# An attention and token-mixing block on one core: raw projection weights for the first two chunks, statistics, norms and weight scalings on any of three engines, and another instruction order

## The chip, the core and the metric

The kernel runs on one core of a Trainium2 chip. The metric is the device time of one execution in microseconds. The engines are PE (TensorE: matmuls, and transposes as matmuls), PEld (its weight loads, which overlap it), DVE (VectorE), ACT (ScalarE), POOL (GpSimd) and SP (SyncE, which here only issues DMAs; its queue shows as SPq). Each engine works through its own queue in order and waits for others by semaphores.

## What is computed

x has 2048 rows (tokens) of 512. Six vectors (sa, ca, ga, sb, cb, gb) come from `silu(c) @ w_mod`. Then:

```
h = layernorm(x) * (1 + ca) + sa
x = x + ga * attention(h)          # 32 heads of 16; each row sees itself and 7 rows before it, 2 apart
h = layernorm(x) * (1 + cb) + sb
x = x + gb * mixer(h)              # layernorm, then an MLP across the 2048 rows: w1 to 1792, gelu, w2 back
```

Attention projects h with wqkv to q, k and v, forms 8 logits per row and head, takes a softmax over them, weights 8 rows of v and projects with wo. Everything in and out is bfloat16.

## The kernel before

Rows lie in 16 tiles of 128. Attention works in five chunks of 2, 4, 4, 4 and 2 tiles (256, 512, 512, 512, 256 rows). `build_chunk` (line 616) creates the operations of a chunk; every operation has a name, and the names are used below.

- `ld_x...` load x, `ld_wqkv0/1/2` the weights of q, k and v (512 KB each), `ld_wmod...` those of the six vectors. `modcols1` and `a1col` make the column 1 + ca, `modcols0` and `sab` the column sa.
- `ln1s` (line 370) is a tile's mean and variance: bn_stats and bn_aggr on DVE, or two accumulating passes on ACT and a short DVE operation `ln1v`. `rstd` takes the inverse deviation on ACT for a group of tiles, `nb` on DVE the matching shift, `n1_t` (`ln_norm`, line 404) normalizes tile t into the tile `h`. The same three steps stand for the second norm (`ln2q`, `ln2m`, `n2_t`) and the third (`ln3s`, `h3_t`); `aff` between them applies cb and sb with two DVE operations.
- `tr` transposes the normalized tiles of chunks 0 and 1 on PE into PSUM and `hT` copies them out; chunks 2 to 4 are transposed by DMA (`xt`).
- `wsc{t}_{kt}` (`scale_w`, line 435) multiplies a quarter of a q, k or v weight matrix by 1 + ca into `w_qkv`. The shift by sa goes through `qvb`, a bias column per projection.
- `qkv{ch}_{t}{j}` projects (t is 0 for q, 1 for k, 2 for v), `ev` evicts the result. `vd` are DMAs that spread v.
- `qk` (DVE) multiplies q by the 8 shifted k, `red` (PE) sums over a head, `max`, `sub`, `exp`, `esum`, `rcp` and `smB` are the softmax, `a2` are DMAs that spread its result, `pv` (DVE) multiplies it by v, `pvacc` (PE) sums, `oev` evicts, `wo` projects, `x1` writes the new x. A qk or pv product of a 512-row chunk is one DVE operation on 4096 elements per partition with both inputs in SBUF (the tile `big`).
- `mlp1` multiplies by w1, `park` keeps partial sums, `padd` and `gelu` finish, `mlp2` multiplies by w2 and `fin` writes out.

The order of the work is written out by hand in the string `ORDER` (lines 182 to 238): a list of the names, in which each engine finds its own queue. A suffix chooses the engine (`:a` ACT, `:d` DVE, `:p` POOL), `:q` splits each matmul of an operation into four that use 32 columns each, and `fill` and `warm` are matmuls without a use, put where PE would stand idle. `schedule` (line 85) turns the string into instructions and gives out the buffers: six PSUM banks, four `big`, five `vD`. Which engine a norm runs on was fixed by three strings of letters, `NE`; which statistics ran on ACT by `LN1A`; which weight scalings on POOL by `VPOOL`.

All operations are recorded by one helper, so that the profile shows them under one line (L133); its rows are told apart by the tiles they write and read.

Of the kernel before, what the change touches and what calls it, by code (L numbers as in the profile page):

```python
# [187 lines left out]
hT1_3:a qkv0_00 sab ev0_12:d n1_6 ld_wmod4 qvb0 ln1s14 ld_wo1 qkv0_02 qvb_cp0 ln1s15 ev0_00:a wsc2_2 qvb1
wsc2_0:d qkv1_00 wsc2_3 ev0_10:a ev0_02:d ln1s10 wsc2_1:d qkv1_10 qvb_cp1 qk0_0 ev1_10:a qkv0_22 qk0_1 n1_7
qkv0_20 ln1s13 qk0_2 qkv1_02 xt6 red0_0 ev1_00:a qk0_3 red0_1 red0_2 ev0_22:a ld_wmod5 qkv1_22 qk1_0 ev0_20:a  # L190
qkv1_12 ev1_02:a vd0_1 red0_3 ev1_12:a mask qkv1_11 vd0_0 ln1s11 max0 xt8 qk1_2 qkv1_01 ev1_11:a sub0 qkv1_03
ev1_01:a xt9 exp0 qkv1_13 qk1_1 ev1_03:a xt7 esum0 ev1_13:a qkv1_20 rcp0 vd0_2 ln1s12 qkv1_21 smB0 qk1_3 a2_0_3
modcol2 rstd1_4 qkv1_23 a2_0_0 ev1_22:a a2_0_2 halo_v1:a red1_0 ev1_20:a a2_0_1 red1_1 ln1v10 ln1v12 ln1v11
ln1v13 nb1_4 red1_2 rstd1_3 n1_15 ld_wo3 red1_3 nb1_3 ld_wo2 mcols0 n1_11 n1_10 qkv2_00 max1 ev1_21:a n1_14 xt10
qkv2_02 ev2_00:a pv0_0 qkv2_10 n1_12 ld_wo0 pv0_1 qkv2_11 vd0_3 ev2_10:a ev2_02:a qkv2_12 qk2_0 n1_13 qkv2_01
xt12 ev2_12:a pvacc0_0 ev2_01:a sub1 qk2_2 xt13 qkv2_03 exp1 qkv2_13 xt11 ev2_11:a ev2_03:a qkv2_22 qk2_1
ev2_13:a esum1 ev1_23:a qkv2_21 rcp1 vd1_2 red2_0 smB1 ev2_21:a ld_b2 red2_1 qk2_3 halo_v2:a a2_1_1 red2_2
# [10 lines left out]
warm3 n2_2 ev4_10:a ln3s0 wo6 a2_3_0 n2_3 ln3s1 a2_3_1 rstd2_4 wo7 x1_6 vd3_1 aff2 rstd3_0 a2_3_2 biascols wo9:q
ev4_20:a a2_3_3 nb2_4 nb3_0 ln3s3 n2_5 n2_4 vd3_2 warm1 ln3s2 h3_1 h3_0 qkv4_12 aff4 rstd3_2 wo8 x1_7 ld_w2_0
nb3_2 ln3s5 h3_3 h3_2 ln2q6 ln3s4 mlp1_0_6_0 ev4_12:a pv3_0 mlp1_0_3_0 x1_9 rstd3_4 mlp1_0_5_0 x1_8 mlp1_0_0_0  # L210
biascols_cp:a ln2q8 nb3_4 pv3_1 halo_v4:a mlp1_0_2_0 h3_4 vd4_1 h3_5 mlp1_0_1_0 ln2q9 pv3_2 ld_w2_1 mlp1_0_2_4
vd4_2 ln2q7 mlp1_0_0_4 vd4_0 mlp1_0_3_4 park0_0:a mlp1_0_1_4 mlp1_0_5_4:q park0_1:a ln2m6 vd4_3 pv3_3 park0_2:a
pvacc3_0 pvacc3_1 oev3_0:a ld_w1_0_1152 pvacc3_2 oev3_1:a mlp1_0_4_0:q rstd2_6 oev3_2:a qk4_2 pvacc3_3 park0_3:a
mlp1_0_7_0 oev3_3:a nb2_6 qk4_1 n2_6 mlp1_0_6_4 mlp1_0_4_4 n2_8 qk4_0 wo12:q ld_w1_0_1408 n2_7 n2_9 qk4_3 wo10:q
park0_4:a aff6 x1_12 red4_0 wo13:q ld_w2_3 park0_5:a ln2q12 red4_1 red4_2 x1_10 red4_3 wo11:q max4 ln2q10 ln3s9
x1_13 sub4:q mlp1_0_8_0:q exp4 ln3s8 ln2q13 mlp1_0_11_0 esum4 ln3s7 rcp4 mlp1_0_12_0 park0_6:a ln3s6 x1_11
mlp1_0_10_0 smB4 rstd3_6 ln2m12 a2_4_2 mlp1_0_9_0 h3_7 rstd2_12 h3_6 a2_4_3 ln2q11 h3_9 mlp1_0_8_4 ln2m13 a2_4_0
nb2_12 ln2m11 n2_12 mlp1_0_7_4 a2_4_1 ln2m10 h3_8 rstd2_10 ld_w2_4 aff12 mlp1_0_9_4 rstd2_13 rstd2_11 nb2_10
ln3s12 mlp1_0_9_8 mlp1_0_7_8 n2_10 mlp1_0_8_8 nb2_13 pv4_0 park0_7:a mlp1_0_12_4 ld_w1_0_1664 park0_8:a
mlp1_0_11_4 nb2_11 pv4_2 n2_13 mlp1_0_10_4 rstd3_12 pv4_1 park0_9:a mlp1_0_12_8 n2_11 mlp1_0_10_8 pv4_3 inj1_4  # L220
mlp1_0_11_8 ld_w1_1_0 park0_10:a pvacc4_2 ld_w1_1_640 park0_11:a pvacc4_0 nb3_12 aff11 pvacc4_1 h3_12 pvacc4_3
mlp1_0_13_0 aff10 oev4_0:a oev4_2:a aff13 mlp1_0_13_4 ln3s10 wo15 ld_w2_5 ln3s13 rstd3_10 mlp1_0_13_8 wo14 x1_15
rstd3_13 park0_12:a inj1_0 nb3_13 ln2s15 mlp1_1_0_6 nb3_10 x1_14 rstd2_15 mlp1_1_4_6 park0_13:a nb2_15 ln2s14
n2_15 inj1_3 inj1_6 ld_w1_1_896 inj1_5 mlp1_1_6_6 rstd2_14 aff15 h3_10 mlp1_1_3_6 ln3s15 mlp1_1_6_10 ln3s11
mlp1_1_0_10 rstd3_15 inj1_1 mlp1_1_1_6 park1_0:a nb3_15 h3_15 n2_14 rstd3_11 aff14 mlp1_1_5_6 h3_13 ln3s14
mlp1_1_5_10 mlp1_1_1_10 inj1_2 ld_w1_2_0 mlp1_1_2_6 h3_11 rstd3_14 park1_1:a h3_14 mlp1_1_4_10 mlp1_1_3_10
# [812 lines left out]
```

## Time and profile before

| | us |
|---|---|
| median of 3 runs | 206.46 (206.19 to 206.73) |
| profiled execution, first to last instruction (span) | 204.6 |
| PE busy | 194.7 |
| DVE busy | 163.3 |
| ACT busy | 120.6 |
| POOL busy | 13.0 |
| first projection matmul starts | 13.61 |
| first qk product starts (DVE) | 19.48 |
| last pv product ends (DVE) | 123.0 |
| last matmul ends | 201.6 |

The profile shows the profiled execution as its span; it gives no other time for it, and the median of the runs is 1.9 us above the span. A row of busy tenths cuts the span into 40 slices of 5.1 us; a 9 is 90% or more. In a timeline the columns are start, duration, engine, line, operation, tile written <- tiles read, shape and count; in brackets stands how long the engine was idle before it and what ended that. In a list of waits the columns are who waited for whom, the total, how often, and the longest. A table by stretches gives the stretch, its length, the busy time of the engine with its count of instructions, PE's granted clock, the busy share of the DMA engines, and GB/s.

### The profile page before, as it was taken

The numbers are of one execution on the slowest core, as the hardware profiler recorded it, in microseconds if no ns is written. First come the engines' busy times: TensorE is split into PE (matmuls) and PEld (weight loads), VectorE is DVE, ScalarE is ACT, GpSimd is POOL, SyncE is SP. The second block draws the span as 40 slices with busy tenths as digits, with TensorE's granted clock in tenths as the row PEclk, the third lists the DMA queues.
The fourth block names the chain that finished last, engine by engine and source line by source line (L and its number), as shares of the span: only waits on it lengthen the run. The fifth ranks groups of instructions, "written<-read, shape, count | busy, mean of one in ns | idle before, by whom it ended". The sixth has DMA issues, their size and how long they took to land.

```text
span 204.6 us, 4223 instructions
## 1 busy us (share of the span) xinstructions
PE 194.7 (95%) x1655; PEld 103.5 (51%) x1655; DVE 163.3 (80%) x260; ACT 120.6 (59%) x283; POOL 13.0 (6%) x36
## 2 busy tenths in 40 slices
PE   3999999999999997989899999999999999999994
PEld 3988554454455553554344445444444444444453
DVE  2899999999999999999999999975473204369365
ACT  2398998994666899989898876683762000000000
POOL 4122001100000001240000000100000000000000
PEclk9999999999999999999999999999999999999999
DMA  5999494646958976194975179946990930121121
GB/s 141 330 380 348 117 239 107 161 98 201 247 186 267 308 234 251 25 272 110 289 200 115 26 157 263 288 131 200 340 304 3 232 88 16 39 77 51 51 82 51
DMA packets 55111, 35.93 MB, mean 176 GB/s; under 512 B 24628, under 2 KB 52404, under 8 KB 55092
## 3 DMA queue, kind: packets, MB, share of 16 engines
q1 hardware_dynamic: 55084, 35.67, 61.4%
q8 instruction: 13, 0.21, 0.4%
q14 instruction: 6, 0.05, 0.1%
q10 hardware_dynamic: 8, 0.00, 0.0%
HBM read 22.55 MB, written 2.10 MB: 121 GB/s over the span
## 4 chain that ended last, share of the span: by engine, by line
PE 65%; DVE 20%; issue 5%; DMA 5%; SPq 3%; ACT 2%; DVEq 0%
PE psS L133 62%; DVE big L133 9%; DVE h L133 3%; PE psL L133 3%; SPq L133 3%; DVE st L133 3%; DMA wst<-in_B_w_dram 2%; DMA xx<-in_A_x_dram 2%; ACT h L133 1%; DVE mv L133 1%; DVE m L133 1%; DVE lsb L133 1%; DVE ls L133 0%; DVE nb L133 0%; DVE woq L133 0%
## 5 line engine op out<-in xcount | busy, mean ns | idle before, releaser
L133 PE MATMUL psS<-h,wst 128*128 128x512 bf16 (+1 forms) x254 | 50.7, 379 | 1.2 <-POOL h L133 0.7
L133 PE MATMUL psS<-hT,w_qkv 128*128 128x512 bf16 (+3 forms) x312 | 46.2, 339 | 0.3 <-ACT w_qkv L133 0.3
L133 PEld LDWEIGHTS <-wst 128*128 128x128 bf16 (+1 forms) x356 | 28.7, 98 | 32.2 <-issue 3.2
L133 PEld LDWEIGHTS <-w_qkv 128*128 128x128 bf16 (+1 forms) x354 | 29.5, 111 | 21.3 <-issue 3.2
L133 DVE TENSOR_TENSOR big<-a2sb,vD 128x4096 bf16<-128x4096 bf16 (+1 forms) x20 | 36.9, 1876 | 0.0
L133 DVE TENSOR_TENSOR big<-q_sb,k_f 128x4096 bf16<-128x4096 bf16 (+1 forms) x20 | 36.3, 1857 | 0.0
L133 DVE SCALAR_TENSOR_TENSOR h<-psS,bcol,rows_bc 128x512 f32<-128x512 f32 (+2 forms) x18 | 12.4, 690 | 24.4 <-PE psS L133 24.2
L133 PE MATMUL psS<-gT,big 128*128 128x512 bf16 x112 | 24.8, 379 | 0.0
L133 PEld LDWEIGHTS <-big 128*128 128x128 bf16 x144 | 12.0, 97 | 13.2
L133 PEld LDWEIGHTS <-ident 128*128 128x128 bf16 (+1 forms) x203 | 13.9, 111 | 5.9 <-issue 2.8
L133 PE MATMUL psS<-woq,o_sb 128*32 128x512 bf16 (+1 forms) x172 | 16.6, 380 | 0.0
L133 ACT ACTIVATE h<-xx,nb,rs 128x512 bf16<-128x512 bf16 x19 | 15.0, 807 | 0.8 <-DVE nb L133 0.7
L133 DVE TENSOR_TENSOR psS<-psS,gT 128x512 f32<-128x512 f32 x14 | 9.3, 696 | 7.0 <-PE psS L133 7.0
L133 ACT ACTIVATE junk<-xx 128x512 bf16<-128x512 bf16 x22 | 13.8, 626 | 0.2
L133 POOL TENSOR_SCALAR h<-xx,rs,nb 128x512 bf16<-128x512 bf16 x9 | 7.3, 813 | 101.3 <-DVE nb L133 84.0
L133 ACT ACTIVATE lv<-mv,epscol 128x1 f32<-128x1 f32 (+2 forms) x25 | 7.3, 291 | 9.3 <-DVE mv L133 8.4
L133 DVE BATCH_NORM_STATS2 st<-xx 128x6 f32<-128x512 bf16 x14 | 9.5, 678 | 4.0 <-DMA xx<-in_A_x_dram 4.0
L133 ACT ACTIVATE gT<-psS,bcol 128x512 bf16<-128x512 f32 x14 | 8.7, 688 | 6.4 <-DVE psS L133 6.4
L133 PEld LDWEIGHTS <-group 128*32 128x32 bf16 x288 | 6.8, 96 | 10.2 <-issue 4.8
L133 DVE TENSOR_TENSOR h<-h,rows_bc 128x512 bf16<-128x512 bf16 (+2 forms) x20 | 11.5, 581 | 0.5
L133 DVE TENSOR_TENSOR h<-h,xx 128x512 bf16<-128x512 f32 (+2 forms) x18 | 11.4, 633 | 0.6
L133 ACT ACTIVATE gT<-psS 128x512 bf16<-128x512 f32 x19 | 10.8, 587 | 1.6 <-PE psS L133 1.5
(94 smaller groups left out, 220.4 us busy)
## 6 DMA issues: line engine op xcount, KB each, us to landing
vD<-v_sb SPq DMA_DIRECT2D x12, 524.5 KB, 3.8
big<-in_B_w_dram SPq DMA_DIRECT2D x4, 896.0 KB, 8.2
vD<-v_sb SPq DMA_DIRECT2D x8, 268.5 KB, 3.0
wst<-in_B_w_dram SPq DMA_DIRECT2D x3, 640.0 KB, 5.3
out_dram<-h SPq DMA_DIRECT2D x15, 128.0 KB, 1.8
xx<-in_A_x_dram SPq DMA_DIRECT2D x7, 256.0 KB, 6.1
wst<-in_B_w_dram SPq DMA_DIRECT2D x2, 800.0 KB, 4.8
gT<-in_w_mod_dram SPq DMA_DIRECT2D x3, 512.0 KB, 6.1
```

The source lines that it names most:

```text
L133: r = fn(*a, **k)
```

## The change

Four things change. The projections of chunks 0 and 1 use the raw weights as loaded (`wraw`), and for these chunks 1 + ca is multiplied into the transposed tiles by the copies `hT`, which so need `a1col`; the scaled weights are still made, for chunks 2 to 4. Statistics of the first and third norm can run on DVE or ACT, norms and weight scalings on DVE, ACT or POOL, each as its name in `ORDER` says; bn_aggr becomes an operation of its own (`ln1v`, `ln2v`, `ln3v`), and the norm on DVE that took mean and deviation without `nb` is gone. The raw v weights lie in the other `h2` buffer. And the whole of `ORDER` is another one: 34 operations carry `:q` instead of 19, on PE the 70 and 16 fillers of the start become 30, 24, 12 and 10, and POOL is given 10 norms of the first kind, 9 of the second and 8 of the third, 7 weight scalings and 2 halo copies (before: 5, 4 and 2 norms, 2 scalings and 1 halo copy).

```diff
-                k, n = map(int, rest)
+                n = int(rest[0])
+                k = min((freed["ps"][i], i) for i in range(self.pools["ps"]) if held["ps"][i] is None)[1]
...
-consts ld_x_1_2 act_table ld_x0 ld_x_1_4 ld_c ld_x_2_8 ld_x1 ident ld_x_2_6 ld_wmod1 ln1s3 halo0 ld_wqkv1 cps
-ln1s2 warm2 ld_wqkv0 silu_exp ld_wmod0 ln1s0 ln1s4 ln1s1 ln1s5 rstd1_0 ld_x_4_14 nb1_0 ln1s9 rstd1_1 n1_0 n1_1
-silu_dve nb1_1 ld_wqkv2 ln1s8 fill:2:70 tr0_0 n1_2 n1_4 modcols1 ln1s7 hT0_3:a n1_5 n1_3 ld_x_3_10 hT0_2:d a1col
-hT0_0:a fill:4:16 tr1_2 wsc1_2:d ld_b1 hT0_1:a wsc1_3:d wsc1_0:a tr1_0 wsc1_1:d ln1s6 hT1_2:a ld_wmod2 qkv0_10
...
+ident ld_x_1_4 ld_x0 act_table ld_x_1_2 ln1s4:d ln1s0:d fill:30 ld_x1 ld_wmod1 ld_c fill:24 cps fill:12 fill:10
+ln1s5:a ln1s3:a ln1s1:d ld_wqkv1 ln1v1 ln1v0 rstd1_0 ln1s2:d nb1_0 ln1v5 ln1v4 silu_exp n1_0:a n1_1:p ln1v3 silu_dve
+modcols1 ln1v2 rstd1_1 nb1_1 n1_5:p n1_4:a ld_wqkv0 a1col wsc0_0:p tr0_0 hT0_0:a n1_2:d ld_x_2_6 n1_3:d consts tr1_0
+ld_wmod0 hT1_1:a tr1_2 hT1_2:a wsc0_2:p ld_x_2_8 hT0_3:d hT0_2:d halo0 hT0_1:d ld_wqkv2 wsc0_1:a ld_b1 hT1_3:d
+wsc1_2:a hT1_0:d wsc1_0:d qkv0_12 qkv0_10 ev0_12:a qkv1_10 ln1s7:d ev0_10:d ln1v7 modcols0 ln1s6:a sab:a ln1s8:d
+qkv0_02 ln1s9:d ev1_10:a qvb0 ld_wo2 ld_wmod2 ln1v6 ln1v8 qvb_cp0:d ln1v9 rstd1_2 wsc1_1:p qkv0_00 qkv1_02 ev0_02:d
+ld_wo0 ld_x_3_10 ld_x_3_12 nb1_2 qk0_3 qvb1 qkv0_22 qkv0_20 ev0_00:a ld_b2 qk0_0 n1_8:a qk0_1 qkv1_12 n1_9:p n1_6:p
+qk0_2 qvb_cp1:a wsc2_0:a ev0_22:a ev1_02:a xt6 modcol2 red0_0 red0_1 ln1s13:d n1_7:p ev0_20:a vd0_3 mcols0 qkv1_11:q
+qkv1_00:q ev1_12:a ln1s10:a wsc0_3:p qk1_2 ln1s11:a red0_2 red0_3 wsc2_3:p ev1_00:a vd0_2 xt9 xt7 mask max0 mrowt0
+qkv1_13 ln1v11 ln1v10 wsc2_1:p mrows0:a st_row0 sub0 ev1_11:a exp0 wsc1_3:p qk1_0 qkv1_01 ev1_01:a xt8 ld_row0
+qkv1_03:q ln1s12:a esum0 rcp0 qk1_1 ev1_13:a qkv1_21:q ev1_03:a ln1v12 vd0_1 ln1v13 rstd1_3 red1_0 ld_x_4_14 smB0
+a2_0_1 qk1_3 qkv2_00:q qkv2_10:q ev2_10:a nb1_3 n1_13:p ev2_00:a qkv2_11:q ev2_11:a a2_0_3 qkv1_23 ev1_23:a wsc2_2:a
+red1_1 red1_2 red1_3 ev1_21:a a2_0_0 vd0_0 a2_0_2 qkv1_20 ev1_20:a qk2_0 qkv1_22 ld_wmod3 ev1_22:a max1 sub1 qkv2_23
+qkv2_03 halo_v1:p n1_11:p pv0_2 pvacc0_2 ld_wo1 exp1 esum1 ev2_23:a rcp1 biascols biascols_cp:a ln1s15:a pv0_3 qkv2_01
+ev2_01:a pvacc0_3 ld_wo3 pv0_0 pvacc0_0 pv0_1 pvacc0_1 oev0_0:a n1_10:p qkv2_13 ev2_13:a smB1 qkv2_02:q ev2_02:a
...
+pv2_0 ev4_02:a ev3_22:a warm3 warm1 n2_5:p aff0 exp3 warm0 qkv3_20 ev3_20:a vd3_3 vd3_0 rstd2_2 nb2_2 pvacc2_3
+oev2_3:a pvacc2_0 oev2_0:a qkv4_10:q ln3s1:a pvacc2_1 qkv4_12 pv2_2 aff4 oev2_1:a ln3s0:a ln3v0 qkv4_20 pvacc2_2 ln3v1
+oev2_2:a esum3 rcp3 ld_w1_0_512 vd3_2 n2_3:p n2_2:p aff2 rstd3_0 nb3_0 smB3 h3_0:p a2_3_2 ln3s3:d warm2 ev4_20:a
+ln3s2:d ln3v3 ln3v2 ln3s5:d wo8:q ln3s4:a ev4_12:a a2_3_1 h3_1:p wo7 rstd3_2 nb3_2 h3_2:p a2_3_0 wo9:q ev4_10:a x1_8
+a2_3_3 ln3v4 ln3v5 rstd3_4 h3_3:d qk4_3 nb3_4 vd3_1 x1_9 halo_v4:d vd4_2 h3_5:d ld_w2_2 pv3_0 h3_4:a wo6:q mlp1_0_0_0
...
+mlp1_0_0_4 pv3_3 mlp1_0_3_0 park0_0:a mlp1_0_1_4 rstd2_6 nb2_6 n2_7:p park0_1:a n2_8:p mlp1_0_2_0 mlp1_0_2_4 park0_2:a
+pvacc3_1 mlp1_0_3_4:q oev3_1:a pvacc3_0 oev3_0:a n2_9:p pvacc3_3 mlp1_0_4_0:q mlp1_0_4_4:q pv3_2 qk4_1 pvacc3_2
...
+nb2_13 n2_13:d aff13 nb2_12 mlp1_0_8_4 mlp1_0_8_8 rstd2_11 nb2_11 mlp1_0_9_0 mlp1_0_9_4 mlp1_0_9_8 n2_12:p a2_4_0
+pv4_2 pv4_0 inj1_1 ld_w1_0_1664 park0_8:a park0_9:a ln3s13:a inj1_5 mlp1_0_10_4 mlp1_0_12_8 mlp1_0_10_8 park0_10:a
...
-    NE=('PAPAAPAADAAPAAPD', 'PAPAAPAAAADAAADP', 'APPAAADDDDADAADA'),
-    LN1A=(10, 11, 12, 13),
+    RAW=(0, 1),
...
-    VPOOL=(2, 3),
...
     def ln_stats(l, st, src, reads, name):
         st6, mv = ln_t["st6", l], ln_t["mv", l]
-        if l == 0 and st in LN1A:
-            def fa():
-                nc.scalar.activation(junk[:], src, ACT.Identity, scale=1.0 / D, accum_out=mv[:, st, 0:1])
-                nc.scalar.activation(junk[:], src, ACT.Square, scale=D ** -0.5, accum_out=st6[:, st, 0:1])
-            add("act", 1.36, fa, reads=reads + ["act_table"], writes=[("sq", l, st)], name=name)
-            add("dve", 0.15, lambda: nc.vector.scalar_tensor_tensor(
-                mv[:, st, 1:2], mv[:, st, 0:1], mv[:, st, 0:1], st6[:, st, 0:1], op0=ALU.mult, op1=ALU.subtract,
-                reverse1=True), reads=[("sq", l, st)], writes=[("mv", l, st)], name="ln1v" + name[4:])
-            return
 
         def fd():
             nc.vector.bn_stats(st6[:, st, :], src)
-            nc.vector.bn_aggr(mv[:, st, :], st6[:, st, :])
-        return add("dve", 0.86, fd, reads=reads, writes=[("mv", l, st)], name=name)
+
+        def fa():
+            nc.scalar.activation(junk[:], src, ACT.Identity, scale=1.0 / D, accum_out=mv[:, st, 0:1])
+            nc.scalar.activation(junk[:], src, ACT.Square, scale=D ** -0.5, accum_out=st6[:, st, 0:1])
+        o = G.add_any([("dve", 0.68, fd)] + ([("act", 1.26, fa)] if l != 1 else []),
+                      reads=reads + (["act_table"] if l == 0 else []), writes=[("stt", l, st)], name=name)
+
+        def fv():
+            if o.eng == "dve":
+                nc.vector.bn_aggr(mv[:, st, :], st6[:, st, :])
+            else:
+                nc.vector.scalar_tensor_tensor(mv[:, st, 1:2], mv[:, st, 0:1], mv[:, st, 0:1], st6[:, st, 0:1],
+                                               op0=ALU.mult, op1=ALU.subtract, reverse1=True)
+        add("dve", 0.15, fv, reads=[("stt", l, st)], writes=[("mv", l, st)], name=name[:3] + "v" + name[4:])
 
...
-        if vreads is None and NE[l][g0:g0 + n] == "D" * n:
-            return
...
     def ln_norm(l, g0, n, st, dst, src, reads, writes, name, by_sums=False):
-        rs, nb, mv = ln_t["rs", l], ln_t["nb", l], ln_t["mv", l]
-        r_, n_, e = rs[:, st, 0:1], nb[:, st, 0:1], NE[l][st]
-        reads = reads + [("rs", l, g0)]
-        with_nb = by_sums or NE[l][g0:g0 + n] != "D" * n
-        reads.append(("nb", l, g0) if with_nb else ("mv", l, st))
-        args = (r_, n_, ALU.mult, ALU.add) if with_nb else (mv[:, st, 0:1], r_, ALU.subtract, ALU.mult)
-        alts = {"A": ("act", 0.8, lambda: nc.scalar.activation(dst, src, ACT.Identity, scale=r_, bias=n_)),
-                "D": ("dve", 0.42, lambda: nc.vector.tensor_scalar(dst, src, args[0], args[1], op0=args[2], op1=args[3])),
-                "P": ("pool", 0.8, lambda: nc.gpsimd.tensor_scalar(dst, src, args[0], args[1], op0=args[2], op1=args[3]))}
-        G.add_any([alts[e]], reads=reads, writes=writes, name=name, locks=True)
+        r_, n_ = ln_t["rs", l][:, st, 0:1], ln_t["nb", l][:, st, 0:1]
+        G.add_any([("act", 0.8, lambda: nc.scalar.activation(dst, src, ACT.Identity, scale=r_, bias=n_)),
+                   ("dve", 0.42, lambda: nc.vector.tensor_scalar(dst, src, r_, n_, op0=ALU.mult, op1=ALU.add)),
+                   ("pool", 0.8, lambda: nc.gpsimd.tensor_scalar(dst, src, r_, n_, op0=ALU.mult, op1=ALU.add))],
+                  reads=reads + [("rs", l, g0), ("nb", l, g0)], writes=writes, name=name, locks=True)
 
...
-            wst[0][:, 0:KT * D].rearrange("p (k n) -> p k n", k=KT), h2_r[0][:, 0:KT, :])
-    wkey = ([("wst", 2)], [("wst", 0)], [("h2", 0, i) for i in range(MT)])
+            wst[0][:, 0:KT * D].rearrange("p (k n) -> p k n", k=KT), h2_r[1][:, 0:KT, :])
+    wkey = ([("wst", 2)], [("wst", 0)], [("h2", 1, i) for i in range(MT)])
...
             alts = [("dve", 0.36, lambda d_=d_, s_=s_, a_=a_: nc.vector.tensor_scalar_mul(d_, s_, a_)),
-                    ("act", 0.7, lambda d_=d_, s_=s_, a_=a_: nc.scalar.activation(d_, s_, ACT.Identity, scale=a_))]
-            if t == 2 and kt in VPOOL:
-                alts = [("pool", 0.8, lambda d_=d_, s_=s_, a_=a_: nc.gpsimd.tensor_scalar(
-                    d_, s_, a_, 0.0, op0=ALU.mult, op1=ALU.add))]
+                    ("act", 0.7, lambda d_=d_, s_=s_, a_=a_: nc.scalar.activation(d_, s_, ACT.Identity, scale=a_)),
+                    ("pool", 0.8, lambda d_=d_, s_=s_, a_=a_: nc.gpsimd.tensor_scalar(
+                        d_, s_, a_, 0.0, op0=ALU.mult, op1=ALU.add))]
             G.add_any(alts, reads=wkey[t] + ["a1col"], writes=[("w_qkv", t, kt)], name=f"wsc{t}_{kt}")
...
-                    copy2(hT[:, kt, :], lambda s_=s_, k2=k2: ps(s_).bitcast(BF)[:, k2 * C:(k2 + 1) * C], C, True, [],
-                          [("hT", bh, kt)], f"hT{ch}_{kt}", frees=s_)
+                    hs = lambda s_=s_, k2=k2: ps(s_).bitcast(BF)[:, k2 * C:(k2 + 1) * C]
+                    hd, a_ = hT[:, kt, :], a1col[:, kt:kt + 1]
+                    if ch not in RAW:
+                        copy2(hd, hs, C, True, [], [("hT", bh, kt)], f"hT{ch}_{kt}", frees=s_)
+                        continue
+                    G.add_any([("act", _t_act(C, 1), lambda hd=hd, hs=hs, a_=a_: nc.scalar.activation(
+                        hd, hs(), ACT.Identity, scale=a_)),
+                               ("dve", 0.12 + 0.00052 * C, lambda hd=hd, hs=hs, a_=a_: nc.vector.tensor_scalar_mul(
+                                   hd, hs(), a_))], reads=["a1col"], writes=[("hT", bh, kt)], name=f"hT{ch}_{kt}",
+                              frees=s_)
...
-                        lhsT = _ap(w_r[t][:, kt, j:j + 1], [[4, P]])
+                        lhsT = _ap((wraw if ch in RAW else w_r)[t][:, kt, j:j + 1], [[4, P]])
...
-                reads=hkeys + [("w_qkv", t, kt) for kt in range(KT)] + [("hT_raw", bh)], alloc=s_,
+                reads=hkeys + (wkey[t] if ch in RAW else [("w_qkv", t, kt) for kt in range(KT)]) + [("hT_raw", bh)],
+                alloc=s_,
```

More of the change, by code (lines that the diff above doesn't have):

```diff
@@ L188 @@
[L188 to L197, printed above, removed]
@@ L208 @@
[L208 to L217, printed above, removed]
@@ L218 @@
[L218 to L226, printed above, removed]
-mlp1_1_2_10 mlp1_1_9_10 park1_2:a ld_w1_1_1408 park1_3:d mlp1_1_7_10 padd1_9 park1_4:a park1_5:d mlp1_1_8_10
@@ L550 @@
     add("pe", 0.42, lambda: f_cols(0), reads=["sc", ("wmodA", 0), "wmA1"], frees=s_wm, alloc=s_m[0], name="modcols0")
-    add("dve", 0.15, lambda: nc.vector.tensor_copy(sab[:], ps(s_m[0])[:, 0:KT]), frees=s_m[0], writes=["sab"],
-        name="sab")
+    copy2(sab[:], lambda: ps(s_m[0])[:, 0:KT], KT, False, [], ["sab"], "sab", frees=s_m[0])
     scale_w(1)
```

56 lines of the change are left out of this document (33 added, 23 removed).

## The prediction

> **What bounds the kernel now.** I read the page first, then the waits, then the timeline of each engine, and the sums follow the timeline.
>
> ```profile
> PE 194.7 (95%) x1655; PEld 103.5 (51%) x1655; DVE 163.3 (80%) x260; ACT 120.6 (59%) x283; POOL 13.0 (6%) x36
> ...
> PE   3999999999999997989899999999999999999994
> ...
> DVE  2899999999999999999999999975473204369365
> ACT  2398998994666899989898876683762000000000
> POOL 4122001100000001240000000100000000000000
> ```
>
> PE is busy throughout, and DVE is full from slice 3 to slice 24. POOL is nearly empty. Until 13.6 us PE's busy time is mostly fillers; its first projection shows in the timeline:
>
> ```profile
> 13.61 1.94 PE L133 MATMUL psS<-hT,w_qkv 128*128 128x256 bf16 x16 [0.26 <-ACT w_qkv L133]
> ```
>
> It waited for a scaled weight. From there PE works until 201.6, and its idle times after 60 us add up to 3.5 (0.09 at 67, 0.74 at 79.7, 0.57 at 81.4, 0.22 at 82.2, 0.68 at 91.5, 0.73 at 101.6, 0.52 at 112.8). Most of them wait for DVE, directly or one step on:
>
> ```profile
> PE psS L133 <- DVE big L133: 1.0, 2, 0.7
> ...
> PE psL L133 <- DVE m L133: 0.7, 1, 0.7
> PE psS L133 <- POOL h L133: 0.7, 1, 0.7
> ```
>
> So the span is 13.6 (start) + 184.5 (PE's work) + 3.5 (waits) + 3.0 (last `fin` and store) = 204.6. The profiled execution is 204.6; the median of the runs is 206.46, and I carry the 1.9 between them unchanged.
>
> DVE is the second chain. Its attention stretch runs from the first qk product (19.48) to the last pv product (123.0): of 103.5 us it is busy 102.2, as the table by stretches says (the second row is POOL's in the same stretch):
>
> ```profile
> 19.48:123.00 103.52, 102.20 (x130) 1.00 0.67 182
> ```
> ```profile
> 19.48:123.00 103.52, 6.27 (x8) 1.00 0.67 182
> ```
>
> To see how tightly the two run, sum the start-to-start durations down both queues. At pv4's last product DVE comes out 3.4 us behind PE, and PE's measured waits are 3.5. So every microsecond added to this DVE stretch is a microsecond of the end.
>
> **The change, part by part.**
>
> *Start.* Chunks 0 and 1 no longer wait for the twelve `wsc` scalings. New chain: x1 is the fourth load instead of the fifth, 256 KB fewer ahead, at the 300 GB/s of these slices 0.85 us, so its 7.33 becomes 6.4. Then bn_stats 0.7 and two short ops to 7.3; ACT has done two statistics (1.4 each, from its `junk` pairs) by 7.4; rstd 0.5, nb 0.1: 8.0. Norms n1_0 and n1_1 end at 9.0. DVE does silu until 9.0, PE modcols1 (0.54), a1col at 9.85; the second group's nb at 9.75, n1_4 and n1_5 end at 10.75, n1_2 and n1_3 on DVE at 10.65. tr1_0 and tr1_2 (0.55 each) stand ahead of qkv0_12 in PE's queue: 11.9. n1_2 on DVE may be held while POOL does n1_5 (0.75): 12.6. I take 12.2, that is 1.4 earlier. hT copies now wait for a1col (9.85), which is no later than their transposes (10.1); behind wsc0_0, which waits on POOL for the third 512 KB load (about 11), stand the constants (1.65), wsc0_2 and halo0, none needed before 20 us. On SP, wmod1 stands behind 640 KB instead of 1280 KB.
>
> *PE's work.* One filler moves from the idle start into the middle (0.5 a piece from 83.69 to 84.19). Runs of 32-column matmuls alternate with full ones 41 times instead of 35; a quad group followed by a full one takes 0.99 (61.90 to 62.89), by a quad one 0.86 (68.43 to 69.29): 6 x 0.13 = 0.8. Work 184.5 + 0.5 + 0.8 = 185.8.
>
> *DVE's stretch.* Off: ln3s of tiles 0, 1, 4, 6 to ACT (0.80 less 0.13 each, 2.7), ln3s12 after the stretch (0.8), one norm (0.4). On: ln1s13 (0.7), ln3s10 (0.7), one park (0.7), aff10 and aff13 for aff12 (0.8), a halo and two small ops (0.4): 0.6 less, 102.9. The eight weight scalings and six of the first statistics leave DVE ahead of the stretch, so the first qk product comes when ev0_02 and nb1_2 are done: PE 12.2 + 4.6 (qvb0), evict and copy to 18.0. Last pv product: 120.9 instead of 123.0. PE's own sum reaches it at 120.2; the largest lag on the way is 1.0 (pv3_2). Waits then fall from 3.5 to 1.0.
>
> *ACT.* It was busy 88.1 of these 103.5. It loses some ten norms (0.71) and gains six ln3s (1.38) and a few scalings, about even; the evictions keep half a microsecond to a few behind PE, as before. Cost nothing; without that cover it is PE's PSUM slots that fill.
>
> So without friction: 12.2 + 185.8 + 1.0 + 3.0 = 202.0, or 203.9 as a median.
>
> *POOL.* Here the change adds what DVE's sum does not show. In the stretch POOL goes from 8 instructions to 27: 25 norms and scalings of 0.7 to 0.8 and two halos. Two places in the trace show what POOL and DVE do to each other:
>
> ```profile
> 36.01 0.77 POOL L133 TENSOR_SCALAR h<-xx,rs,nb 128x512 bf16<-128x512 bf16 x1
> ```
> ```profile
> 36.28 1.57 DVE L133 TENSOR_TENSOR big<-a2sb,vD 128x2048 bf16<-128x2048 bf16 x1
> ...
> 49.49 1.21 DVE L133 TENSOR_TENSOR big<-a2sb,vD 128x2048 bf16<-128x2048 bf16 x1
> ```
> ```profile
> 83.95 1.15 POOL L133 TENSOR_SCALAR h<-xx,rs,nb 128x512 bf16<-128x512 bf16 x1 [4.48 <-DVE nb L133]
> ```
>
> A pv product that met a norm on POOL took 1.57 instead of 1.21, 0.36 more. A norm that met DVE's smB (83.77 to 84.45) took 1.15 instead of 0.77. Beside bn_stats or a reduction from PSUM (78.69, 87.55, 88.30) norms ran at 0.77 and cost nothing. Before, most of the other six fell in such places. In the new order I count 13 that become ready amid DVE's products: n1_9, n1_6, n1_7, wsc2_3, wsc1_3, n1_11, n1_10, n1_12, n2_4, n2_5, n2_7, n2_8, n2_9. Of the other twelve, eight have bn_stats, a max or esum4 beside them, and n2_3, n2_2, n2_12 and h3_2 stand where DVE's next operation needs them or is short. Bounds: nothing, if each finds a gap; 0.7 each, if DVE loses all of it. I take the measured 0.36 to 0.38, the only rows there are: 13 x 0.37 = 4.8. Span 206.8, median **208.7**.
>
> [...]
>
> The clock: fillers ran 12 in each microsecond up to 8.5 and about 24 from 9.0, under a granted clock of 1.00 throughout. Now they start at 1.5 (ident is first on POOL) and end near 7.8, then PE pauses until modcols1. If the pace fell back, 128x256 matmuls at twice their 0.12 would cost 16 x 0.12 = 1.9; modcols1 and the transposes lie between, so I take nothing. [...]
>
> **Rivals.**
> 1. *Norms find gaps* (32%). For: DVE waits now and then (1.3 us in the stretch), and PE has new slack of 2.4 us. Against: POOL's 19 us must fit beside some 14 us of DVE work that leaves it alone. At most 5 of the 13 collide: 203.9 to 205.8, faster.
> 2. *Products take about 0.37 per meeting* (40%), my forecast: 206.5 to 211 (7 to 19 meetings). It outweighs the gain of 2.6 from the eighth meeting on (7 x 0.37 = 2.6).
> 3. *DVE loses the whole norm* (13%): 13 x 0.7 = 9.1, so 213.0. For: two instructions that alternate would do it. Against: 0.36 measured of 0.50 left.
> 4. *DVE keeps going and POOL waits* (10%). Then seven POOL jobs must be done before qkv2_00, which PE reaches at 29.7 (12.2 + 17.5); ln1s13 and max0 let two through, the other five run when DVE runs dry at 33.4, ending 37.3: 7.6 late, 211.5. For: smB held a norm for 0.38.
> 5. *The raw weights buy nothing* (5%): chunk 1's transposes ahead in PE's queue, held by n1_2 and a late load, keep qkv0_12 at 13.6. Then 1.4 more on the forecast: 210.1.
>
> **How the numbers follow.** 208.7 is the second case. 203.9 to 212.8 leaves out what of the first case is better than no meeting at all and the third case, under 2 in 10 together; the second case alone is 206.5 to 211. About 0.3% (0.6 us) is what can be told from no change: below 205.8 lies case 1 but for its edge, faster 0.31; 205.8 to 207.1, the low end of case 2, 0.08; slower 0.61.
>
> **What would show it.** First qkv matmul at 12.2 (11.9 to 12.6); first qk product at 18.0. Products of 128x2048 and 128x4096 longer than 1.22 and 2.28 just where a POOL norm lies, their excess some 5 us in sum; PE's waits some 6 us, named DVE big and DVE m. If products keep 1.22 and 2.28 and norms keep 0.77, case 1 holds. If norms grow to 2 us and PE waits near 30 us for w_qkv or hT, case 4. I am wrong altogether if the last pv product ends at 121 us or before.

## The result, and the profile after

The changed kernel takes **215.49 us** (median of 4 runs, 214.50 to 216.66), the kernel before, beside it, 206.34 (206.19 to 206.73). The ratio is 1.043, with a 95% interval from 1.037 to 1.049: slower, and 2.7 us above the top of the range of the prediction (212.8). The profiled execution took 216.46; its span is 214.7. Ratios in this document leave out executions that a slow state of the chip lengthened, and of the profiles shown only that of `late_dve` is such an execution.

The page of the changed kernel: busy time, and slices of 5.4 us.

```profile
PE 198.9 (93%) x1858; PEld 104.1 (48%) x1858; DVE 161.6 (75%) x248; ACT 124.4 (58%) x307; POOL 60.8 (28%) x58
...
PE   7689993999999999896999999999999999999993
...
DVE  2569998499899999999979989983673406632684
...
POOL 1183999600133006864083207140000000000000
PEclk9969998899999999998899999999999999999999
```

POOL's row, mostly zeros before, has grown to nines; PE and DVE, nearly without a gap before, have a hole in the seventh and the eighth slice; and TensorE's clock, 1.00 throughout before, shows three dips. The costliest group of POOL tells more than its share: a norm of 128x512 took 0.81 on average. This is its line before, and behind it the lines of the changed kernel:

```profile
L133 POOL TENSOR_SCALAR h<-xx,rs,nb 128x512 bf16<-128x512 bf16 x9 | 7.3, 813 | 101.3 <-DVE nb L133 84.0
```
```profile
L134 POOL TENSOR_SCALAR h<-xx,rs,nb 128x512 bf16<-128x512 bf16 x19 | 37.5, 1978 | 64.8 <-DVE nb L134 63.9 <-DVE a1col L134 0.9
L134 POOL TENSOR_SCALAR w_qkv<-h,a1col 128x512 bf16<-128x512 bf16 x2 | 8.1, 4046 | 0.0
```

Now a norm takes 1.98 us on average, and two weight scalings 4.05. Where they lie shows in POOL's timeline, with DVE's beside it:

```profile
19.84 8.42 POOL L134 TENSOR_SCALAR h<-xx,rs,nb 128x512 bf16<-128x512 bf16 x3 [4.51 <-DVE nb L134]
28.24 0.68 POOL L134 TENSOR_SCALAR w_qkv<-wst,a1col 128x512 bf16<-128x512 bf16 x1
28.91 8.07 POOL L134 TENSOR_SCALAR w_qkv<-h,a1col 128x512 bf16<-128x512 bf16 x2
```
```profile
19.71 5.04 DVE L134 TENSOR_TENSOR big<-q_sb,k_f 128x2048 bf16<-128x2048 bf16 x4
24.68 0.68 DVE L134 BATCH_NORM_STATS2 st<-xx 128x6 f32<-128x512 bf16 x1
...
28.85 4.48 DVE L134 TENSOR_TENSOR big<-q_sb,k_f 128x4096 bf16<-128x4096 bf16 x2
33.26 0.64 DVE L134 SCALAR_TENSOR_TENSOR mv<-mv,st 128x1 f32<-128x1 f32 x1
...
40.48 2.49 DVE L134 TENSOR_TENSOR big<-q_sb,k_f 128x4096 bf16<-128x4096 bf16 x1 [3.49 <-ACT q_sb L134]
```

The three norms took 3.84, 1.72 and 2.88, the two scalings 4.99 and 3.11. They are long while products run back to back, and a scaling that meets none (28.24) takes 0.68. Together the 25 norms and scalings of the attention stretch took 50.0 us; at 0.77 each it would be 19. DVE pays too, but mostly in small operations that come up behind a POOL read: the `mv` at 33.26 takes 0.64, elsewhere (97.97) 0.21. PE's waits, in total, times and longest:

```profile
PE psS L134 <- DMA hT<-h: 3.7, 2, 3.5
PE psS L134 <- POOL h L134: 1.9, 1, 1.9
PE psS L134 <- DVE big L134: 1.4, 3, 1.0
```

The longest one stands in PE's timeline. It is the third chunk's first projection, waiting for its transposed tiles:

```profile
35.77 4.32 PE L134 MATMUL psS<-hT,w_qkv 128*32 128x512 bf16 x48 [3.50 <-DMA hT<-h]
```

**Where the 10.1 us of span lie.** All in the attention stretch, from the first qk to the last pv product. These figures are the profiled executions' own; behind the last pv product every kernel here has 80.6 to 82.0 us left.

| kernel | first qk | last pv ends | stretch | DVE busy in it | DVE idle in it |
|---|---|---|---|---|---|
| before | 19.48 | 123.0 | 103.5 | 102.2 | 1.3 |
| changed | 19.71 | 134.0 | 114.3 | 106.3 | 8.0 |
| changed, POOL reads nothing (`no_read`) | 19.59 | 124.5 | 104.9 | 101.2 | 3.7 |
| before, with 13 more norms on POOL (`before_pool`) | 19.35 | 132.6 | 113.3 | 104.3 | 9.0 |

The changed kernel's row of the table, as the profile gives it:

```profile
19.71:134.01 114.30, 106.28 (x131) 0.97 0.63 170
```

PE's sum says the same: from the first projection (13.23) to the last matmul (211.3) it was busy 189.9 (before 184.4) and idle 8.2 (3.6). Of the 5.5 more work, 1.3 are the filler and the 32-column runs of the forecast; the rest is clock (below).

### The profile page after: what moved, and what is told of

Its sections match the earlier page's. It is cut to its first block, busy times and chain, and to the rows that moved or that the text cites. A ratio compares the mean times of both kernels' runs of the same rounds, so it can differ in the third digit from the quotient of the medians.

```text
span 214.7 us, 4663 instructions
## 1 busy us (share of the span) xinstructions
PE 198.9 (93%) x1858; PEld 104.1 (48%) x1858; DVE 161.6 (75%) x248; ACT 124.4 (58%) x307; POOL 60.8 (28%) x58
## 4 chain that ended last, share of the span: by engine, by line
PE 52%; DVE 28%; POOL 5%; DMA 5%; issue 3%; ACT 3%; SPq 2%; DVEq 0%; ACTq 0%
PE psS L134 51%; DVE big L134 17%; POOL h L134 5%; DVE h L134 4%; DMA xx<-in_A_x_dram 2%; DMA hT<-h 2%; DVE st L134 2%; SPq L134 2%; DVE mv L134 2%; DVE m L134 1%; PE psL L134 1%; DMA a2sb<-lsb 1%; DVE lsb L134 1%; DVE nb L134 1%; ACT lv L134 1%
## 5 line engine op out<-in xcount | busy, mean ns | idle before, releaser
L134 POOL TENSOR_SCALAR h<-xx,rs,nb 128x512 bf16<-128x512 bf16 x19 | 37.5, 1978 | 64.8 <-DVE nb L134 63.9
L134 PEld LDWEIGHTS <-wst 128*128 128x128 bf16 (+1 forms) x474 | 36.5, 103 | 37.7 <-issue 6.9
L134 PE MATMUL psS<-h,wst 128*128 128x512 bf16 (+1 forms) x272 | 52.4, 386 | 1.9 <-POOL h L134 1.9
L134 PE MATMUL psS<-hT,w_qkv 128*32 128x512 bf16 (+3 forms) x372 | 30.9, 366 | 4.1 <-DMA hT<-h 3.7
L134 PEld LDWEIGHTS <-w_qkv 128*32 128x32 bf16 (+1 forms) x414 | 20.6, 111 | 21.9 <-issue 9.3
L134 ACT ACTIVATE junk<-xx 128x512 bf16<-128x512 bf16 x30 | 18.9, 629 | 2.2 <-DMA xx<-in_A_x_dram 1.7
L134 PEld LDWEIGHTS <-ident 128*128 128x128 bf16 (+2 forms) x211 | 11.9, 105 | 6.2 <-issue 2.0
L134 DVE TENSOR_TENSOR h<-h,xx 128x512 bf16<-128x512 f32 (+2 forms) x18 | 11.4, 633 | 3.8 <-DMA out_dram<-h 3.1
L134 ACT ACTIVATE v_sb<-psS,qvb 128x512 bf16<-128x512 f32 (+1 forms) x20 | 11.4, 603 | 2.5 <-PE psS L134 2.4
L134 PE MATMUL psS<-hT,wst 128*32 128x512 bf16 (+2 forms) x100 | 12.6, 359 | 0.0
L134 POOL TENSOR_SCALAR h<-h,rs,nb 128x512 bf16<-128x512 bf16 x8 | 7.7, 966 | 14.5 <-DVE mv L134 8.1
```

Of the source, the lines that this page charges most:

```text
L134: r = fn(*a, **k)
```

## The experiments

The theory after the result: **(1)** a POOL instruction that reads SBUF gets in only now and then between DVE's products; it is late, and what waits for it holds PE, which stops DVE in turn. Rivals: **(2)** the new order itself costs the time (its 32-column runs, the places of its statistics); **(3)** the cold clock of the start sets everything late. Ratios are to the kernel before, run on the same chip; "us" is the ratio times 206.3, so that runs on different chips can be compared (the changed kernel is 215.3 in this measure).

| run | ratio (95%) | us |
|---|---|---|
| `early_off` | 1.030 (1.024 to 1.036) | 212.5 |
| `late_off` | 1.101 (1.096 to 1.107) | 227.2 |
| `all_off` | 1.091 (1.086 to 1.096) | 225.1 |
| `late_dve` | 1.068 (1.058 to 1.078) | 220.3 |
| `head_fill` | 1.037 (1.030 to 1.044) | 213.9 |
| `no_read` | 0.994 (0.990 to 0.998) | 205.1 |
| `no_read_early` | 1.018 (1.014 to 1.022) | 210.1 |
| `no_read_late` | 1.017 (1.011 to 1.022) | 209.7 |
| `no_read_fill` | 0.996 (0.994 to 0.999) | 205.6 |
| `raw_only` | 1.000 (0.997 to 1.003) | 206.4 |
| `before_pool` | 1.048 (1.040 to 1.056) | 216.3 |
| `wsc_early` | 1.041 (1.035 to 1.046) | 214.7 |
| `wsc_early_n3` | 1.027 (1.023 to 1.030) | 211.8 |
| `wsc_early_n3h` | 1.025 (1.022 to 1.028) | 211.5 |

**POOL's reads taken out.** In `no_read`, norms and scalings of the stretch write a constant on POOL (the profile counts 21 norms and 4 scalings, not the 18 and 4 of the expectation):

```diff
-("pool", 0.8, lambda: nc.gpsimd.tensor_scalar(dst, src, r_, n_, op0=ALU.mult, op1=ALU.add))
+("pool", 0.8, lambda: nc.gpsimd.tensor_scalar(dst, src, r_, n_, op0=ALU.mult, op1=ALU.add)
+    if name in ("n1_1", "n1_5", "h3_10", "n2_14", "h3_11", "h3_13") else nc.gpsimd.memset(dst, 0.01))
...
```

> The changed kernel in which GpSimd, from 19 us to the end of the attention stretch, fills the outputs of its 18 norms and 4 weight scalings with a constant (a memset of the same 128x512) and reads nothing: those norms and scalings are left out. Order, engines and all other work are as in the changed kernel. A memset here waits for no mean or deviation, so GpSimd is never late. Theory 1 (reads of GpSimd wait for VectorE's products, their lateness holds PE and its clock): memsets take some 0.2 to 0.4 us, PE's idle time falls from 8.2 to about 3.6 us and the clock falls at 36 and 100 us go (3.1 us): 207.8 us (206.5 to 209.5). Theory 2 (the order itself): 213 or more. Were it my forecast's mechanism (VectorE's products lengthened), the products would now have to be shorter than in the changed kernel, where they already have 1.22 to 1.26 and 2.29; no change from that.

205.1: the whole loss goes, and a little more, and it is below the range that I had expected. Nothing else was changed, so the order itself is not what costs (rival 2 falls), and its granted clock at 12 to 14 us was 0.50 as in the changed kernel (rival 3 falls). Its POOL rows (0.52 for a memset, not the 0.2 to 0.4 expected), and the stretch of DVE:

```profile
L134 POOL MEMSET h<- 128x512 bf16 x21 | 10.1, 522 | 27.7 <-ACT junk L134 21.0 <-ACT h L134 6.7
```
```profile
19.59:124.49 104.90, 101.21 (x131) 1.00 0.71 183
```

The memsets also wait for no mean or deviation (the row names ACT where the changed kernel's has DVE's `nb`), so the run does not separate the reads from those waits. The next two runs keep the reads; and the 50.0 us above are the instructions themselves, without their waits for semaphores.

**The disputed cost by itself.** `port` is a kernel of its own that computes nothing of the block:

```diff
+    gate()                                # a tiny DVE operation that POOL waits for
+    norms(8)                              # POOL: 8 x tensor_scalar 128x512, SBUF to SBUF
+    for i in range(10):
+        prod(i, 4096)                     # DVE: tensor_tensor, both inputs in SBUF
```

> The disputed cost by itself: a kernel that computes nothing of the block. In nine phases, each behind a small gate on both engines, GpSimd normalizes 128x512 tiles from SBUF: A alone; B beside ten back-to-back products of 128x4096 on VectorE, C beside sixteen of 128x2048, D beside 2048-products and bn_stats in turn, E beside eight 128x4096 operations with one SBUF input, F beside twelve 128x512 products with one input in PSUM; G GpSimd memsets beside products; H ScalarE norms beside products; I products alone. Theory 1 (the products keep going, a norm gets in only when VectorE pauses or turns to another kind of work): norms 0.7 in A, E and F, over 2 us in B and C, 0.7 to 1.3 in D; products 2.28 and 1.22 or some 0.4 longer only where a norm got in; G and H undisturbed. My forecast's theory: norms near 0.77 to 1.15 and each product that meets one 0.37 longer, so B and C end 3 us later for eight norms. Third rival (the two alternate): each product followed by one norm, starts of products 0.7 further apart.

POOL's timeline, one line for each of the phases A to F (four norms, then eight each; F's is the last):

```profile
11.54 2.69 POOL L134 TENSOR_SCALAR h<-xx,g 128x512 bf16<-128x512 bf16 x4 [10.25 <-DVE g L134]
14.51 26.05 POOL L134 TENSOR_SCALAR h<-xx,g 128x512 bf16<-128x512 bf16 x8 [0.28 <-DVE g L134]
40.85 21.43 POOL L134 TENSOR_SCALAR h<-xx,g 128x512 bf16<-128x512 bf16 x8 [0.28 <-DVE g L134]
62.56 11.57 POOL L134 TENSOR_SCALAR h<-xx,g 128x512 bf16<-128x512 bf16 x8 [0.28 <-DVE g L134]
74.41 13.37 POOL L134 TENSOR_SCALAR h<-xx,g 128x512 bf16<-128x512 bf16 x8 [0.28 <-DVE g L134]
88.06 5.36 POOL L134 TENSOR_SCALAR h<-xx,g 128x512 bf16<-128x512 bf16 x8 [0.28 <-DVE g L134]
```

Alone a norm takes 0.67 (A), as beside products with one input in PSUM (F: 5.36 / 8). Beside products of 4096 it takes 4.8. Single instructions of phase B, DVE's and POOL's:

```profile
18.74 2.70 DVE L134 TENSOR_TENSOR big<-a2sb,vD 128x4096 bf16<-128x4096 bf16 x1
```
```profile
19.28 4.84 POOL L134 TENSOR_SCALAR h<-xx,g 128x512 bf16<-128x512 bf16 x1
```

One norm for every **two** products: 4.84 is about what two products take from start to start, 2.20 and 2.62, and every second product takes 2.70 instead of 2.28. Beside products of 2048 (C) it is 2.70 for each norm, and every second product 1.62 instead of 1.21. Beside a product and bn_stats in turn (D) a norm takes 1.75, one for each bn_stats, and the products keep 1.21. Memsets took 0.52, with products beside them or not, ScalarE's norms took 0.72, and both left the products at 2.28. So both theories of a price were half right: DVE pays 0.41 for each read that gets in, near my 0.37, **and** POOL waits for up to two products. Three points were missed: the regular turn, every second boundary; phase D, where I had expected 0.7 to 1.3; and phase E. There, beside `tensor_scalar` of 128x4096, with one SBUF input, norms also took 2.65 to 2.70, until DVE had ended, and then 0.69. The product that meets a norm in B loses 0.42, not the norm's whole 0.67. Why a norm gets in at every second boundary only, and why the operation of E, with its one SBUF input, is met in the same way, no run shows.

**The other part in the old order.**

```diff
-    NE=('PAPAAPAADAAPAAPD', 'PAPAAPAAAADAAADP', 'APPAAADDDDADAADA'),
+    NE=('PAPAAPPPDPPPPPPD', 'PAPPPPAPPPDAPADP', 'PPPAAADDDDADAADA'),
```

> The other part alone: the kernel before, in its own order, with 13 more norms of the attention stretch on GpSimd instead of ScalarE, each that the changed kernel has there (n1_6, 7, 9, 10, 12, 13; n2_3, 4, 7, 8, 9, 12; h3_0). By theory 1 those beside products take 2.3 to 4.8 us, and the transposes, second norms and MLP tiles behind them come late: PE's waits grow from 3.5 to 8 or more, named hT, DVE or POOL h, and the time is 210 to 216. By my forecast (0.37 a meeting for VectorE and nothing else): at most 13 x 0.37 = 4.8 less ScalarE's relief: 206.5 to 211, norms near 1.15. If the reads cost only in the new order: 206.3.

216.3, as much as the whole change. POOL's, PE's and DVE's timelines of it show the same chain. Of five norms in a row (11, 10, 14, 12, 13) the first three take 0.76 to 0.77, and the last two, beside products, 4.91 and 5.43; the next chunk's projection is late, and DVE runs dry.

```profile
35.10 12.56 POOL L133 TENSOR_SCALAR h<-xx,rs,nb 128x512 bf16<-128x512 bf16 x5 [15.96 <-DVE mcols L133]
```
```profile
51.53 3.58 PE L133 MATMUL psS<-hT,w_qkv 128*128 128x512 bf16 x8 [3.62 <-DMA hT<-h]
```
```profile
57.27 1.22 DVE L133 TENSOR_REDUCE m<-psL 128x128 bf16<-128x1024 f32 x1 [5.15 <-PE psL L133]
```

The raw weights alone, on the other hand, are worth nothing there:

```diff
+lhsT = _ap((wraw if ch in (0, 1) else w_r)[t][:, kt, j:j + 1], [[4, P]])
...
+nc.vector.tensor_scalar_mul(hd, hs(), a_)
...
-... hT0_2:d a1col hT0_0:a ...
+... modcols1 a1col ln1s7 hT0_3:a ... hT0_2:d hT0_0:a ...
```

> One part alone: the kernel before, in its own order and with its own engines, but with raw weights for the projections of chunks 0 and 1, 1 + ca multiplied in by the copies of the transposed tiles, and a1col moved ahead of the first of these copies. If the raw weights are worth something by themselves, the wait of 0.26 us for the first scaled weight goes and the first projection starts at 13.3 instead of 13.6; the scalings stay in their places on VectorE: 206.0 to 206.5 against 206.3. If the copies with a1col come late instead (VectorE and ScalarE queues), 207.

Ratio 1.000; the first projection came at 13.12 in its profiled execution, the first qk product at 19.29 (before 19.48): DVE was busy without a gap from 14.8 to there, so its queue, not the projection, sets that.

**Early or late reads.** The same constants for only the seven POOL operations ahead of the third chunk, or only the 18 later:

> The changed kernel in which only the seven GpSimd operations ahead of the third chunk (norms of tiles 9, 6 and 7, four weight scalings) are replaced by constants, so that these norms and scalings are left out. If the early reads are the greater part (PE's wait of 3.5 at 32, the fall of the clock behind it of 1.5, VectorE's lengthening there): 210 us or less, 5.5 of the 9.2 us that no_read gains. If the later 18 are: 213 or more. If the two overlap (each delay hidden by the other), neither half gains as much as its share: the two gains add up to less than 9.2.

> The counterpart: only the 18 later norms of GpSimd in the stretch are replaced by constants and left out. PE's wait of 1.9 at 98 and the low clock behind it (1.6), VectorE's wait for n2_2 and the lengthening of its work there: 211 to 212, 4 of the 9.2 us. PE's wait of 3.5 us at 32 stays.

5.2 and 5.6 us: about even, and together (10.8) no less than `no_read` gains (10.2). Neither hides the other. Both profiled executions also had a warm start (1.00 at 12 to 14, see below) and their first projection at 11.3 and 11.4, which the changed kernel's had not; a part of each gain may be the start's, for which `head_fill` has 1.4.

**Moving them to other engines.** The tokens' engine letters were changed, nothing else:

```diff
-n1_9:p n1_6:p ... n1_7:p ... wsc0_3:p ... wsc2_3:p ... wsc2_1:p ... wsc1_3:p
+n1_9:d n1_6:d ... n1_7:d ... wsc0_3:d ... wsc2_3:d ... wsc2_1:d ... wsc1_3:d
```

> The changed kernel with seven of its GpSimd operations ahead of the third chunk (norms of tiles 6, 7, 9 and four weight scalings) given to VectorE, each at its place in the order. Theory 1 (GpSimd starves beside VectorE's back-to-back products, and what it is late with holds PE): PE's wait of 3.5 us at 32 and the fall of its clock right behind it (1.5 us) go, VectorE does 7 x 0.36 = 2.5 more of which 3.5 us of its own idle time there pay: 210.5 us (209.5 to 212), against 215.5 for the changed kernel. Theory 2 (the new order itself, its 32-column runs and the places of the statistics, costs the time): 215 to 217, PE's wait moves elsewhere. Theory 3 (the cold clock of the start sets everything behind it late): no change, 215.5.

> The changed kernel with the other 18 norms that GpSimd has in the attention stretch given away: ten to ScalarE, eight to VectorE (the engine each had in the kernel before, VectorE where that was GpSimd). Theory 1: PE's wait of 1.9 us at 98, the low clock behind it (1.6 us) and about 1 us of smaller waits go, VectorE does 8 x 0.38 = 3.0 more: 212.5 us (211 to 214.5). Theory 2: 215 to 218, as VectorE and ScalarE only have more to do. Theory 3: no change.

> Both of these at once: GpSimd keeps only the start, the halo copies and the time after the stretch. Theory 1: the gains add up, 207.5 us (206 to 210), and the granted clock stays at 1.00 from 20 us on. Theory 2: 213 to 217. Theory 3: no change, 215.5.

> The changed kernel with the 18 later norms of GpSimd on VectorE (in late_off ten went to ScalarE, where they stood ahead of evictions and waited for their group's deviation, so that all evictions waited with them). Theory 1: PE's wait at 98 and the clock fall behind it go (3.5 us) and about 1 us of other waits, VectorE's stretch gets 18 x 0.38 = 6.8 longer less what POOL lengthened (1.9): 215 to 217. Theory 2: 219 to 222 (the whole 6.8 on top).

`early_off` gained 2.8 of the 5 expected (PE's wait near 32 went, but PE now waited 3.3 for DVE's `max`, DVE having seven operations more); the other three, which I had expected to gain or to lose little, lost 5 to 12. The reason is not POOL's reads, of which these three have fewer: in an in-order queue a norm stands where its token stands. In `late_dve` `n1_14` ran on DVE behind two qk products, at 74.59 instead of 58.31, and the last chunk's projection waited for its transposes (DVE's timeline, then PE's):

```profile
74.59 0.41 DVE L134 TENSOR_SCALAR h<-xx,rs,nb 128x512 bf16<-128x512 bf16 x1
```
```profile
82.11 1.89 PE L134 MATMUL psS<-hT,w_qkv 128*128 128x256 bf16 x8 [4.90 <-DMA hT<-h]
```

In `late_off` and `all_off` PE's waits for the same tiles, 9.9 and 5.4 in sum, point the same way; their other losses I did not follow. Moving an operation without its place therefore told little about its price; leaving its read out did. Three more runs moved four scalings up, to where DVE works on statistics and PSUM (`wsc1_1:p wsc0_3:p wsc2_3:p wsc2_1:p wsc1_3:p`), then also the three norms to DVE with fillers in the start, then also `n2_2:d n2_3:d h3_1:d h3_2:d`:

> The changed kernel with four weight scalings of GpSimd moved up in its queue, to right behind the scaling before them, so that they run from 15.3 us, beside statistics and evictions from PSUM, instead of behind the norms of tiles 9, 6 and 7, beside products. By the measurement of the port alone (a norm gets in at every second boundary of products, 2.70 or 4.84 us; 0.69 beside operations that read PSUM): the scalings take 0.70 each instead of 0.68, 4.99, 3.11 and 0.69. The three norms stay beside products (8.4 us) and the transposes behind them still end near 35.7: PE's wait of 3.5 us stays, and the time is 214 to 215.5. If the scalings were what held PE, the wait goes and the time is 210 to 212.

> As wsc_early, and also the norms of tiles 9, 6 and 7 on VectorE (3 x 0.36) and 35 fillers in the idle times of the start (22, 5 and 8). Theory 1: no GpSimd read is left between 19.7 and 37 us, PE's wait near 32 and the fall of its clock behind it go (5.0), VectorE has 1.1 more, the start gives 0.8: 210 to 211.5. If the third chunk is late for another reason (theory 2): 214.

> As wsc_early_n3, and also the norms n2_2, n2_3, h3_1 and h3_2 on VectorE, which waited for them or ran beside them (4.4 us for two at 89 and 2.0 for two at 98, after which PE waited 1.9 and its clock fell). Theory 1: another 3.5 gone, 1.5 more on VectorE: 208 to 209.5. Theory 2: 214 to 216.

214.7, 211.8 (just above the 210 to 211.5 expected) and 211.5. In the first the scalings took 0.70 each, as expected, and PE's wait stayed (3.1), so the norms held it. In the second that wait was all but gone (0.5) and the granted clock 1.00 throughout. The third took away PE's wait for POOL, as expected, but not its time, a miss of 2 us or more. PE's waits in it:

```profile
PE psL L134 <- DVE m L134: 3.1, 2, 1.6
PE psS L134 <- DVE big L134: 2.2, 5, 1.0
```

DVE, with seven norms more and the reads that are left, is now what comes last: busy 106.4 in a stretch of 110.6. No version here that computes the block was faster than the kernel before.

**The clock.** Three runs bear on it, two with fillers in the start:

```diff
-fill:10 ... tr1_0 ... tr1_2
+fill:10 fill:34 ... fill:5 tr1_0 ... fill:8 tr1_2
```

> The changed kernel with 47 more fillers in the idle times of the start (34 ahead of the first column products, 5 and 8 ahead of two groups of transposes), all else as it is. If the low clock from 11.7 to 16 us (0.50 and 0.74 granted) comes from PE's idle time after 7.6 us, it stays near 1.00 there, the 15 transposes take 1.2 instead of 1.8, the first raw projections 0.12 a matmul instead of 0.18, the first product on VectorE comes 1.3 earlier (18.4), and the time is 214.0 to 214.7. If GpSimd's lateness then still sets the third chunk (theory 1), the rest of the gain is swallowed by PE's wait near 32. If the clock has another cause, nothing changes: 215.5.

> no_read (norms and scalings of GpSimd in the stretch left out) with 35 fillers in the idle times of the start (22, 5 and 8), so that TensorE's clock should be granted 1.00 from 10 to 16 us. If the cold clock costs what the first matmuls lose (20 raw projections and 15 transposes, 1.5 us) and nothing behind swallows it: 204.5 to 205.0 against 206.0 to 206.3. If VectorE's stretch swallows it: no change. My forecast without friction was 203.9.

With fillers the granted clock was 1.00 from 10 to 20 us in all four such profiles. `head_fill` gained 1.4 (the intervals overlap), and `no_read_fill` nothing over `no_read` that can be measured: in the kernel that POOL does not hold, DVE's stretch swallows a warm start. The start itself was a natural experiment: the same order gave a long wait in some executions and a short one in others. PE waits for `sc`, behind the first loads; where this wait was short, the clock stayed. The changed kernel and `no_read_late`, the same start, each with the table by stretches (the granted clock stands behind the count; the second and third row are the falls behind PE's two long waits):

```profile
9.64 0.54 PE L134 MATMUL psS<-sc,big 128*128 128x1 bf16 x16 [2.00 <-DVE sc L134]
```
```profile
12.00:14.00 2.00, 2.00 (x18) 0.50 1.10 379
...
36.00:40.00 4.00, 4.00 (x48) 0.63 0.66 201
...
100.00:104.00 4.00, 3.76 (x10) 0.57 0.92 262
```
```profile
8.58 0.54 PE L134 MATMUL psS<-sc,big 128*128 128x1 bf16 x16 [0.53 <-DVE sc L134]
```
```profile
12.00:14.00 2.00, 1.93 (x16) 1.00 1.10 369
```

Finer stretches say more. They put the changed kernel's three falls at 11.62 to 15.03, 35.52 to 38.93 and 100.37 to 103.78: each is 3.41 us long, and the times between them, 20.5 and 61.4, are 6 and 18 times 3.41. In the 3.41 us ahead of each fall PE was busy 1.24, 0.15 and 1.51. The waits ahead of the first and the third were 2.00 and 1.91, so a wait need not last 3.41 us to be followed by a fall. In `wsc_early`, counted on in steps of 3.41 from its last fall (an estimate, as no fall marks the place), such a stretch ends at 99.97. It holds most of the same wait of 1.91, PE was busy 1.63 in it, and the clock stayed (1.00 from 98 to 104). The busy time does not decide alone, as in `early_off` the clock fell at 11.63 behind 1.84. What does decide, no run shows.

## Why the prediction was wrong

The direction was right, the time 6.8 us too low. By `no_read` this divides into 1.2 to 1.7 in the forecast without friction (203.9; the runs without POOL's reads gave 205.1 and 205.6) and some 5.4 in what POOL's reads cost: 10.2 where I had 4.8.

- **The failed step:** the sum put POOL's own lateness at nothing. It stands in the sentence "I take the measured 0.36 to 0.38, the only rows there are: 13 x 0.37 = 4.8", which is wrong not in its size but in what it leaves out. DVE's busy time in the stretch is 106.3 with the reads and 101.2 without, 5.1 more. Operation for operation, 13 are 0.2 to 0.45 longer, 4.9 in sum, so my count and price held. But that was luck: four of the 13 are products, the others shorter operations; and of the 13 norms and scalings that I named seven took over 1.1 us, as did seven that I had not named. What is missing is the other side of a meeting: POOL's own lateness (2 to 5 us for an operation of 0.7 to 0.8), which stopped PE for 3.5 and 1.9 us, and DVE behind it. DVE's idle time is 8.0 instead of 3.7, another 4.3; with the 5.1 that makes the 9.4 by which the stretches differ.
- The smaller miss, 1.2 to 1.7, is there without the reads too, in the same stretch: DVE was idle 3.7 in `no_read` and 2.8 in `no_read_fill`, where I had left it at 1.3. Why, I did not follow.
- I had set "products take 0.37" and "DVE keeps going and POOL waits" (rival 4, 10%) against each other, as if one excluded the other. Both happen: in `port` DVE lost 0.41 to 0.42 for each norm that got in, and the norms took 2.70 to 4.84. Rival 4 named the place, the sign (norms of 2 us and more, PE waiting near 30 us for hT) and came closest in kind with 211.5, but it counted only the third chunk: the later reads cost as much again (`no_read_late`). Rival 3's 213.0 lies nearer to the time by luck, as DVE lost 0.41 at a meeting and not 0.7.
- The row that I leaned on, a norm of 1.15 that met `smB` at 83.77, was a poor sample: behind that one operation came bn_stats (at 84.37), so the norm had only one boundary to wait for. In a row of products it waits for up to two (4.84 in `port`). The length of the chain that a reader meets should have been counted, not the meeting.
- *"The clock: … I take nothing"* was wrong in this execution: 0.50 at 12 to 14 and 0.74 at 14 to 16 us. Clock missing from 1.00 times busy time gives an estimate of 0.9 us from 13.2 on, and 1.5 and 1.6 behind the two long waits of PE: 4.0, which with the forecast's 1.3 is all but 0.2 of PE's 5.5 us of longer work. The bound of 1.9 for the start held. That `modcols1` and the transposes lie between did not help: they ran from 9.64 on, behind the wait of 2.00, and at 11.62 the clock fell. The fillers ahead of the wait ran at some 11 in each microsecond and rose to 21 by 5 to 6 us. By what rule the clock falls was not shown: the falls keep whole multiples of 3.41 us between them, and a wait of 1.91 us for `h3` was followed by 0.57 in the changed kernel and by 1.00 in `early_off`. I misread the fillers' pace before: it was some 10 and then 21, not 12 and 24. As the row says 1.00 at both, it may not show the clock ahead of that rise.
- *First qkv 12.2, first qk 18.0*: 13.23 and 19.71. The first use of `x1` came at 6.89 instead of 6.4, and `modcols1` ran at 9.64; where it ran at 8.5 to 8.7, the first projection came at 11.3 to 11.5, earlier than forecast. Chance of the loads, not the order, decides here: with the early load the first qk product came at 17.4 to 18.3, near my 18.0. Rival 5, that the raw weights buy nothing, was nearer the truth in the profiled execution than its 5%: 0.4 us at the first projection and nothing at the first qk product; and they bought nothing in `raw_only`.
- *PE's work 185.8* held but for the clock, and so did the 3.0 behind the last matmul (3.4).
